# Four pair copies of Pool ahead of the last routing slot of a period

## The chip, the cores and the metric

The kernel runs on one core of one Trainium2 chip. The metric is the device time of one execution in microseconds (us): the median of several runs. TensorE (PE) multiplies matrices, VectorE (DVE), ScalarE (ACT) and Pool (GpSimd) work element by element, and the sync engine (SP) issues most transfers. Each engine runs its own list of instructions strictly in the order in which it was written, and waits at an instruction whose inputs aren't there yet.

## The reference

Attention inside chunks of 64 tokens, for 8 batches, 8 heads, 576 tokens and 64 values per head, and then a layer of 8 experts. Each token goes to one expert. Its own best one counts where a local gate is under one half; otherwise it takes over the expert of the token before it, so the choice is a running recurrence over the tokens of a batch.

```python
scores = scale * np.matmul(q_c, k_c.transpose(0, 1, 2, 4, 3))
attn = softmax(scores)                      # over the 64 keys of the chunk
x = np.matmul(attn, v_c)                    # then to (batch, token, 512)
...
for s in range(S):
    fresh_e = int(np.argmax(logits[b, s]))
    e = fresh_e if s == 0 or local_gate[b, s] < 0.5 else prev_e
    prev_e = e
    h = np.maximum(x[b, s] @ w1[e], 0.0)
    out[b, s] = p[e] * (h @ w2[e])          # p: softmax of the logits
```

## The kernel before

The 4608 tokens are cut into 18 blocks of 256 (numbers 0 to 17). Attention runs as a software pipeline over them. A *period* is one turn of the loop in line 754, with `i` from 1 to 15, and it works on several blocks at once, each at another stage. The order of the steps of a period is a string of tokens, `PAR["steady"]` in line 60; `play` (line 456) walks over it and issues what each token stands for. The lists of TensorE, VectorE, ScalarE and Pool all stand in exactly this order (`manual_schedule`, line 752), so a step of Pool that is written later runs later.

The tokens that matter here:

- `lq`, `lv`: SP issues the loads of `qt` and `kt` for block i+5 and of `v` for block i+1.
- `pr` (four steps, `a_pair`, line 433, through `pair_heads`): Pool copies `qt` and `kt` of block i+3 into `qr` and `kr`, pairing heads, in two copies each (line 156). `qr` and `kr` have a single buffer.
- `tq` (eight steps): TensorE transposes `qr` and `kr` of block i+2 (line 164), and ScalarE takes the results out of PSUM. So what `pr` of one period writes, `tq` of the next one reads.
- `ra` (two steps, `router`): the logits of block i-2, in lines 284 and 293, with VectorE in between; its last step writes the finished rows to the DRAM tensor `x_d` (line 302).
- `s`, `tp`, `va`, `tx`: scores and softmax, transposes of the probabilities, values (line 242), transposes of the output.
- `h0` to `h3`: four slots of a period, in which a step of the *routing* of the first 9 blocks can be placed.

The routing is the recurrence above for 18 tiles of 128 tokens at a time, then a rank for each token inside its expert, and then the slots that tokens take in the expert tiles. It consists of 18 steps. `PAR["hooks"]` gives each a number; the number divided by 4 is the period and the rest is the slot. So 59 is `h3` of period 14 and 63 is `h3` of period 15. In `h3` stand steps of VectorE or TensorE in periods 10 to 13. In period 14 stand `after_a` (lines 744 to 746, VectorE) and `onehots` (line 421): 18 one-hot matrices `rh`, of which VectorE makes every third and Pool the other twelve, as soon as VectorE has written the ranks `rq` (line 417) in slot `h2`. In period 15 stand the *slot matmuls* (line 559, 18 of them, which read `rh` and VectorE's `qv` of line 551) and the *early gather*: Pool issues three indirect transfers (line 594) that fetch rows of `x_d` for the first three expert tiles. Block 17 is the last, so `pr` does nothing in period 15.

At the end of each period from 8 to 15 Pool also makes one half of a low part of the first expert's weights (line 97), once ScalarE has made the high part.

After period 15 comes the *drain* (`PAR["drain"]`): the rest of attention, the routing of the other 9 blocks and the first three expert tiles, interleaved by hand in one order. Its token `x0` transposes the first gathered tile (line 588). Then follows the expert stage: 46 tiles at most of 128 tokens, each with 24 matmuls of 512 columns for `h` (line 627) and 24 for `y` (line 641).

```python
toks = [t for t in PAR["steady"].split() if opt.get(t.split("*")[0], 1) is not None]
play(" ".join(toks), qs4 | {k: v for k, v in opt.items() if v is not None})
...
dsts = [pe2.tile([P, 4, 2, 2, D], F32, name=nm + "r", tag=nm + "r", bufs=1) for nm in "qk"]
...
return [lambda t=t: rh_eng(t).tensor_scalar(rh[:, t], iota_m, rq[:, 0, t:t + 1], None, ALU.is_equal)
        for t in range(t0, t1)]
```

Of the kernel before, what the change touches and what calls it, by code (L numbers as in the profile page):

```python
# [56 lines left out]
    "t0": "VAVA",  # L57
    "t1": "AAAA",
    "t2": "AVAA",
    "steady": "lq s*8 s h0 tx*8 s va*4 va tq*8 ra*2 h1 tq*8 va*4 lv va ra*2 h2 tp*8 s h3 pr*4 ",  # L60
    "hooks": [43, 43, 46, 47, 49, 50, 51, 51, 53, 54, 55, 55, 58, 59, 59, 62, 63, 63],
}

# [918 lines left out]
```

## Time and profile before

| what | value |
|---|---|
| median of 3 runs | 723.87 us (723.59 to 726.48) |
| the profiled execution | 728.72 us |
| its span, first to last instruction | 726.9 us |
| mean granted TensorE clock | 0.969 of full speed |
| TensorE busy | 661.4 us, 91% of the span |
| Pool busy | 188.1 us, 26% of the span |
| moved by the DMA engines | 97.49 MB, 134 GB/s in the mean |

The profile is of one execution, and its timeline counts from the first instruction. A row of the timeline has the start, the duration, the engine, the line and operation, what is written and read, how many instructions were merged, and in brackets how long the engine sat idle before and what ended that. The periods spoken of below lie near 149 to 156 us (period 14) and 156 to 174 us (period 15), by the matmuls of line 193 with which each begins; the drain follows, and the expert stage fills TensorE from some 230 us on. A row of the windows has the stretch, its length, the busy time and count of each of TensorE's matmuls, its weight loads, VectorE, ScalarE and Pool, then the granted TensorE clock, the DMA engines' busy share and their GB/s.

### The profile page before, as it was taken

What the parts mean: (1) busy time and instruction counts of PE and PEld (TensorE: products, weight loads), DVE (VectorE), ACT (ScalarE), POOL (GpSimd) and SP (SyncE); (2) the same over time, 40 slices, a digit from 0 to 9 for tenths busy, and PEclk for the clock granted to TensorE, in tenths of its full rate; (3) what the DMA queues carried; (4) which work ended last, traced back from release to release, by engine and by line L of the source; (5) the groups of instructions that cost most, each with busy time, mean ns of one, the idle gap of its engine ahead of it and who ended that gap; (6) DMA issues with size and microseconds to landing.
All of it is one profiled execution on the core that took longest, in us unless ns stands there. A gap on an engine that the chain in (4) does not pass through costs nothing. (4 is left out here: it accounts for less than half of the span.)

```text
span 726.9 us, 17103 instructions
## 1 busy us (share of the span) xinstructions
PE 661.4 (91%) x5594; PEld 524.8 (72%) x5594; DVE 362.0 (50%) x852; ACT 272.2 (37%) x432; POOL 188.1 (26%) x230
## 2 busy tenths in 40 slices
PE   4779898777999999999999999999999999999971
PEld 4668676565777788777888887778877888777861
DVE  2547655574685585256232562572576323454310
ACT  3547665554521234341222443422454222432210
POOL 3322233345022132123121231331243212231100
PEclk9989999998999999999999999999999999999986
DMA  9999999996833144145111253441277111333100
GB/s 211 201 200 234 233 240 245 247 254 178 217 102 118 46 148 135 71 146 164 42 46 46 84 164 101 148 156 47 79 239 249 60 44 46 97 111 130 49 19 15
DMA packets 102928, 97.49 MB, mean 134 GB/s; under 512 B 42672, under 2 KB 79536, under 8 KB 102768
## 3 DMA queue, kind: packets, MB, share of 16 engines
q1 hardware_dynamic: 96608, 75.70, 42.1%
q0 software_dynamic: 6160, 19.85, 8.2%
q8 instruction: 78, 1.28, 0.8%
q14 instruction: 82, 0.67, 0.3%
HBM read 76.48 MB, written 19.56 MB: 132 GB/s over the span
## 5 line engine op out<-in xcount | busy, mean ns | idle before, releaser
L641 PE MATMUL y<-w2h,hp 128*128 128x512 f32 x608 | 203.7, 405 | 10.3 <-DVE hp L591 6.3
L627 PE MATMUL h<-w1h,xp 128*128 128x512 f32 x608 | 178.3, 403 | 0.0
L641 PEld LDWEIGHTS y<-w2h,hp 128*128 128x128 f32 x608 | 114.9, 190 | 39.1 <-DVE hp L591 8.9
L627 PEld LDWEIGHTS h<-w1h,xp 128*128 128x128 f32 x608 | 111.4, 189 | 23.9 <-ACTq L863 0.2
L641 PE MATMUL y<-w2l,hp 128*128 128x512 f32 x304 | 121.1, 399 | 0.0
L700 POOL DMA_INDIRECT out<-ysb,sidx x38 | 41.2, 1085 | 273.5 <-DVEq L863 197.4
L627 PE MATMUL h<-w1l,xp 128*128 128x512 f32 x304 | 95.9, 396 | 0.0
L590 ACT CAST hp<-tr 128x512 fp32r<-128x512 f32 x76 | 41.2, 589 | 108.0 <-PE tr L588 97.0
L591 DVE TENSOR_TENSOR xp<-tr,xp 128x512 fp32r<-128x512 f32 x39 | 27.0, 691 | 106.5 <-ACTq L863 67.0
L699 DVE TENSOR_SCALAR ysb<-y,ppr 128x512 f32<-128x512 f32 x35 | 26.2, 747 | 92.7 <-PE y L641 81.7
L627 PEld LDWEIGHTS h<-w1l,xp 128*128 128x128 f32 x304 | 57.0, 188 | 14.7 <-DVEq L863 0.7
L641 PEld LDWEIGHTS y<-w2l,hp 128*128 128x128 f32 x304 | 57.9, 190 | 12.3
L680 ACT ACTIVATE hsb<-h 128x1024 f32<-128x1024 f32 x35 | 35.9, 1027 | 67.5 <-PE h L627 64.9
L591 DVE TENSOR_TENSOR hp<-tr,hp 128x512 fp32r<-128x512 f32 x76 | 49.2, 685 | 13.5 <-ACT hp L590 12.5
L613 ACT ACTIVATE pex<-pex 128x8 f32<-128x8 f32 x38 | 7.9, 209 | 117.2 <-DVE pex L612 117.2
L594 POOL DMA_INDIRECT xg<-x_d,gidx x36 | 36.9, 1026 | 40.7 <-issue 19.3
L97 POOL TENSOR_TENSOR w1l<-raw,w1h 128x512 fp32r<-128x512 f32 (+1 forms) x15 | 27.7, 1844 | 70.6 <-ACT w1h L96 70.6
L242 PE MATMUL o<-v,pT 64*64 64x65 f32 x1152 | 32.0, 235 | 13.5 <-DMA v<-in_v 12.9
L242 PEld LDWEIGHTS o<-v,pT 64*64 64x64 f32 x1152 | 24.6, 143 | 23.0 <-DMA v<-in_v 15.8
L588 PE MATMUL tr<-ident,hsb 128*128 128x128 f32 x304 | 40.3, 273 | 0.3 <-ACT hsb L680 0.3
L97 DVE TENSOR_TENSOR w2l<-raw,w2h 128x1024 fp32r<-128x1024 f32 x21 | 39.9, 1952 | 0.9 <-issue 0.9
L588 PEld LDWEIGHTS tr<-ident,hsb 128*128 128x128 f32 x304 | 35.3, 141 | 6.8 <-ACT w2h L96 1.2
(173 smaller groups left out, 832.5 us busy)
## 6 DMA issues: line engine op xcount, KB each, us to landing
raw<-in_moe_w SPq DMA_DIRECT2D x72, 512.0 KB, 5.0
x_d<-xs SPq DMA_DIRECT2D x18, 521.0 KB, 5.7
v<-in_v SPq DMA_DIRECT2D x72, 128.0 KB, 6.0
qt<-in_q SPq DMA_DIRECT2D x11, 512.0 KB, 6.4
kt<-in_k SPq DMA_DIRECT2D x11, 512.0 KB, 7.6
qt<-in_q SPq DMA_DIRECT2D x6, 256.0 KB, 6.2
kt<-in_k SPq DMA_DIRECT2D x6, 256.0 KB, 6.7
qt<-in_q SPq DMA_DIRECT2D x4, 384.0 KB, 7.0
```

What stands on the lines that cost most here:

```text
L97: (lo_eng or nc.vector).tensor_tensor(lo, raw, hi.bitcast(F32), ALU.subtract)
L242: nc.tensor.matmul(o[64 * cp:64 * cp + 64, cc, DV * h:DV * h + D + 1], pT[64 * cc:64 * cc + 64, 4 * j + h, 64 * cp:64 * cp + 64], vt[64 * ...
L588: nc.tensor.transpose(ps[:, n], src_of(n), ident)
L590: return [tr, lambda: nc.scalar.copy(hi, box["ps"]), lambda: V.tensor_tensor(lo, box["ps"], hi.bitcast(F32), ALU.subtract)]
L591: lambda: V.tensor_tensor(lo, box["ps"], hi.bitcast(F32), ALU.subtract)]
L594: nc.gpsimd.indirect_dma_start(out=dst, out_offset=None, in_=src, in_offset=bass.IndirectOffsetOnAxis(ap=gidx[t].bitcast(U32), axis=0))
L613: lambda: nc.scalar.activation(ex[:, 0], ex[:, 0], AF.Exp),
L627: nc.tensor.matmul(hs[:, j], xs[a][:, c], W1[w][c][:, 512 * j:512 * j + 512], start=(c == 0 and n == 0), stop=(c == 3 and n == 2))
L641: nc.tensor.matmul(y, hx[f // 4][a][:, f % 4], W2[w][c][:, f % 2, :], start=(f == 0 and n == 0), stop=(f == 7 and n == 2))
L680: nc.scalar.activation(hsb, hs.rearrange("p j f -> p (j f)"), AF.Relu)
L699: either(mix, lambda: V.tensor_scalar(ysb, y, pr, None, ALU.mult), lambda: y_mixed(ysb, y, ym, pr))
L700: nc.gpsimd.indirect_dma_start(out=out, out_offset=bass.IndirectOffsetOnAxis(ap=sidx[t].bitcast(U32), axis=0), in_=ysb, in_offset=None, bo ...
```

## The change

In the string for a period the token `pr*4` is put ahead of `h3`. Nothing else is edited.

```diff
-    "steady": "lq s*8 s h0 tx*8 s va*4 va tq*8 ra*2 h1 tq*8 va*4 lv va ra*2 h2 tp*8 s h3 pr*4 ",
+    "steady": "lq s*8 s h0 tx*8 s va*4 va tq*8 ra*2 h1 tq*8 va*4 lv va ra*2 h2 tp*8 s pr*4 h3 ",
```

Pool's list from period 13's weight split (`w1l_76`, line 97) to that of period 14 (`w1l_77`) and the first early gather; `qr` and `kr` are the pair copies of block 17, `rh` the one-hots. It is the only piece of Pool's list that differs:

```order
 L97 TENSOR_TENSOR w1l_76<-raw_2_88,w1h_72 128x512
+L156 COPY qr<-qt 128x4x128 x2
+L156 COPY kr<-kt 128x4x128 x2
 L421 TENSOR_SCALAR rh<-iota_m,rq 128x128 x12
-L156 COPY qr<-qt 128x4x128 x2
-L156 COPY kr<-kt 128x4x128 x2
 L97 TENSOR_TENSOR w1l_77<-raw_3_89,w1h_73 128x512
 L594 DMA raw_0_86<-x_d,gidx_2942 128x521
```

The four copies have moved from behind the twelve one-hots to in front of them; the weight split and the gather stand where they stood.

TensorE's list has the same instructions in the same order. Its semaphore waits differ in period 15, at the slot matmuls of line 559, which read the one-hots `rh`; a rank of Pool's list that TensorE had already waited for need not be waited for again. The start of that piece:

```order
 L559 LDWEIGHTS rh [waits DVE_49]
 L559 MATMUL tr<-qv_0_2896,rh 128x12 [waits Activation_49]
-L559 LDWEIGHTS rh
+L559 LDWEIGHTS rh [waits Pool_49]
+L559 MATMUL tr<-qv_0_2896,rh 128x12
+L559 LDWEIGHTS rh [waits Pool_49]
 L559 MATMUL tr<-qv_0_2896,rh 128x12
```

Each of the twelve weight loads of a one-hot that Pool makes has now a wait for Pool of its own; before, `tq` of the same period had waited for the copies behind all of them. The lists of VectorE, ScalarE and SP have the same instructions in the same order.

## The prediction

> **What bounds the kernel now.** I read the page first, for the engine that carries the span, then the waits of TensorE, then the timelines of the engines named there, and last the granted clock around that place.
>
> ```profile
> PE 661.4 (91%) x5594; PEld 524.8 (72%) x5594; DVE 362.0 (50%) x852; ACT 272.2 (37%) x432; POOL 188.1 (26%) x230
> ```
>
> TensorE is busy for 91% of the span, and nothing else comes near. The chain of waits on the page holds under 2% of the span, so it names no culprit. What TensorE waited for does: first up to 174 us, then from there to the end.
>
> ```profile
> PE o L242 <- DMA v<-in_v: 8.3, 13, 1.2
> PE tr L164 <- POOL qr L156: 5.7, 1, 5.7
> PE tr L559 <- DVE qv L551: 1.2, 1, 1.2
> ...
> PE y L641 <- DVE hp L591: 6.3, 5, 1.8
> PE y L641 <- ACTq L884: 3.7, 1, 3.7
> PE tr L588 <- DMA raw<-x_d,gidx: 1.1, 1, 1.1
> ```
>
> The columns are the sum, the count and the longest. One wait stands out: 5.7 us, once, in front of the transposes of line 164, for Pool's copy into `qr`. From 174 us on the only wait for a transfer is the 1.1 us for the first early gather; the others are for engines whose own work follows TensorE's, and they shift with it.
>
> ```profile
> 260.00:700.00 440.00, 433.41 (x2132) 343.87 (x2130) 208.44 (x416) 149.73 (x226) 108.23 (x86) 1.00 0.33 106
> ```
>
> In the expert stage TensorE has work for 433.41 of 440 us at clock 1.00, with the DMA engines a third busy. Work that starts earlier there ends earlier: no later transfer or engine can take back what the attention stage gains.
>
> **Where the 5.7 us come from.** Pool's timeline, from period 13 to the gathers:
>
> ```profile
> 143.45 1.17 POOL L156 COPY qr<-qt 128x512 f32<-128x512 f32 x2 [3.97 <-issue]
> 146.50 1.17 POOL L156 COPY kr<-kt 128x512 f32<-128x512 f32 x2 [1.88 <-issue]
> ...
> 158.55 7.07 POOL L421 TENSOR_SCALAR rh<-iota_m,rq 128x128 bf16<-128x128 bf16 x12 [6.81 <-DVE qsA L744]
> 165.55 1.17 POOL L156 COPY qr<-qt 128x512 f32<-128x512 f32 x2
> 166.66 1.19 POOL L156 COPY kr<-kt 128x512 f32<-128x512 f32 x2
> 167.80 1.28 POOL L97 TENSOR_TENSOR w1l<-raw,w1h 128x512 fp32r<-128x512 f32 x1
> 175.45 1.19 POOL L594 DMA_INDIRECT raw<-x_d,gidx  x1 [6.37 <-DVE sidx L572]
> ```
>
> Pool sits idle for 6.81 us until VectorE has the ranks, makes twelve one-hots in 7.07 us, and only then does the pair copies of block 17, whose transposes TensorE wants in period 15. TensorE, first in period 14 and then in 15:
>
> ```profile
> 151.84 1.09 PE L164 MATMUL tr<-ident,qr 128*128 128x128 f32 x8
> 152.86 0.64 PE L284 MATMUL lg<-xT,wg 128*32 128x256 f32 x8
> 153.43 1.09 PE L164 MATMUL tr<-ident,kr 128*128 128x128 f32 x8
> ...
> 155.09 0.44 PE L293 MATMUL lg<-ident,lT 128*128 128x128 f32 x2
> ...
> 166.22 1.97 PE L164 MATMUL tr<-ident,qr 128*128 128x128 f32 x8 [5.71 <-POOL qr L156]
> 168.12 1.08 PE L284 MATMUL lg<-xT,wg 128*32 128x256 f32 x8
> 169.13 1.52 PE L164 MATMUL tr<-ident,kr 128*128 128x128 f32 x8
> ...
> 171.21 0.44 PE L293 MATMUL lg<-ident,lT 128*128 128x128 f32 x2
> ...
> 173.76 0.61 PE L559 MATMUL tr<-qv,rh 128*128 128x12 bf16 x18 [1.24 <-DVE qv L551]
> ```
>
> **The change, part by part.** Only Pool's order in period 14 changes: the four copies stand ahead of the twelve one-hots. In the other periods no Pool work stands at this place, or no copy does.
>
> *The stall goes: 5.71 us.* The copies need three things: the landed `qt` and `kt`, and `qr` and `kr` read out by period 14's transposes. Those reads end at 152.93 and 154.52. In period 13 the copy into `kr` at 146.50 followed the same kind of read by about 0.1 us, so I put the new copies at 153.1 to 154.2 and 154.6 to 155.8. The loads are long there:
>
> ```profile
> 139.60 0.43 SPq L125 DMA_DIRECT2D qt<-in_q  x1
> 140.12 1.05 SPq L125 DMA_DIRECT2D kt<-in_k  x1
> ...
> DMA to landing us min/median/max: 5.5/7.6/10.0
> ```
>
> By the slowest landing of a `kt` in this stretch (10.0 us) the second has landed by 151.2. So the copies end near 155.8, in the 6.81 us in which Pool waited anyway: the one-hots still start at 158.55 and end at 165.62, and cost nothing more. TensorE gets to the transposes at 166.22 - 5.71 = 160.51 and finds them fed.
>
> *The slow clock after the stall goes: 1.74 us.* From the first `qr` transpose to line 293 period 15 took 171.21 - 166.22 = 4.99 us, and period 14 took 155.09 - 151.84 = 3.25 us, for the same list of matmuls. The windows show why (the third number from the end is the granted clock):
>
> ```profile
> 150.00:160.00 10.00, 8.89 (x209) 7.23 (x202) 8.50 (x32) 6.74 (x12) 2.73 (x4) 1.00 1.09 272
> 160.00:163.00 3.00, 0.51 (x32) 0.37 (x28) 2.93 (x7) 0.62 (x2) 3.00 (x6) 1.00 1.31 198
> 163.00:170.00 7.00, 3.78 (x20) 2.64 (x21) 0.78 (x2) 1.26 (x2) 6.08 (x10) 0.52 0.70 211
> 170.00:175.00 5.00, 3.76 (x112) 3.27 (x113) 2.71 (x15) 3.68 (x6) 0.00 (x0) 0.99 0.35 79
> ```
>
> The clock drops to about half in the stall and is back near 170. Without the stall I give period 15 the 3.25 us of period 14. [...]
>
> *What is late next.* The sum is 5.71 + 1.74 = 7.45 us at line 293. Behind it the slot matmuls of line 559 waited 1.24 us for VectorE; VectorE's work there follows line 293, so this wait stays and they start at 173.76 - 7.45 = 166.31. They read the one-hots, which end at 165.62: 0.7 us to spare, and I count no wait. But the covering wait is gone. Before, the wait for the later pair copies also said that the one-hots were done; now twelve weight loads wait for Pool one by one. No row has such a wait on TensorE when it is already satisfied; the nearest is a satisfied one of VectorE:
>
> ```profile
> L156 DVEq EVENT_SEMAPHORE  x2: 21/21/21, 5.9 to 20.2; - x2
> ```
>
> Bounds are 0 and the whole duration of the 18 matmuls once more (0.61 us); twelve times 21 ns is 0.25 us, and I take that.
>
> *The transfers get closer together.* Line 137's load of `v` for block 16 and line 302's write follow TensorE, so they move up with it.
>
> ```profile
> 161.71 1.95 SPq L93 DMA_DIRECT2D raw<-in_moe_w  x2
> 171.29 2.67 SPq L137 DMA_DIRECT2D v<-in_v  x4
> ...
> 154.00:168.00 14.00, 7.18 (x159) 6.06 (x157) 7.88 (x29) 5.32 (x9) 9.45 (x17) 0.83 1.05 269
> 168.00:171.00 3.00, 3.00 (x44) 1.90 (x47) 0.42 (x1) 1.38 (x4) 1.08 (x1) 0.66 0.03 11
> 171.00:182.00 11.00, 8.26 (x203) 6.96 (x196) 7.69 (x27) 6.58 (x12) 4.37 (x4) 1.00 0.68 183
> ...
> 180.90 0.63 PE L588 MATMUL tr<-ident,raw 128*128 128x128 f32 x4 [1.06 <-DMA raw<-x_d,gidx]
> ```
>
> Before, the DMA engines were saturated to 168 (269 GB/s), then empty for 3 us. After, `v` is issued at 171.29 - 7.45 = 163.84, into that backlog. Up to 182 there are 11 us at 183 GB/s to move, 2.0 MB; at 269 GB/s they need 7.5 us, and from 168 to the shifted 182 - 7.45 there are 6.6. So some 0.9 us are missing in the worst case that all of it must be there by then. Pool issues the first gather at 175.45 - 7.45 = 168.0, behind its weight split, which then ends near 166.9. TensorE's wait for it was 1.06 us. It can vanish (a gain of 1.06) or grow by the 0.9; a full queue is nearer to the second, and I take 0.5 us of loss.
>
> *Pool beside VectorE.* The copies now run beside VectorE's work of period 14, not alone, and more of VectorE's work falls beside the end of the one-hots. The copies of all periods, most of which ran so, and the twelve one-hots:
>
> ```profile
> L156 POOL COPY kr<-kt x35: 608/617/629, 7.3 to 167.2; 128x512 f32<-128x512 f32 x35
> ...
> L421 POOL TENSOR_SCALAR rh<-iota_m,rq x12: 597/604/641, 158.5 to 165.0; 128x128 bf16<-128x128 bf16 x12
> ```
>
> No copy took over 629 ns and no one-hot over 641: nothing to add. Twelve at 641 would take 7.7 us and end 0.6 later, still inside the margin. [...]
>
> **The sum.** 5.71 + 1.74 - 0.25 - 0.5 = 6.7 us. The profiled execution took 728.72 us (span 726.9): it would take 722.0. The median of the runs is 4.85 us lower, 723.87; the stall is one between engines and should be in those runs too, so I take the same 6.7 us off: **717.2 us**.
>
> **The rivals.** *The transfers take half of it back.* The gather lands behind the backlog and TensorE's wait grows from 1.06 to about 2.9 us (the 0.9 above, and as much for its own bytes in a full queue); that wait could let the clock drop once more, for another 1.74 us. It keeps 7.45 - 0.25 - 1.8 - 1.7 = 3.7 us: 720.2. For it: the 13 waits for `v` in the busy stretch before. Against it: from 160.5 to 163 TensorE was idle and the clock still 1.00, so 2.9 us is barely enough. Chance 0.13.
>
> *The one-hots become the wait.* If VectorE's work slows each by 0.15 us, they end 1.8 us later than 165.62, and line 559 waits 1.1 us: 718.3. It bites from 0.7 us on. Chance 0.08. Against it: the row above.
>
> *Nothing is gained.* Period 15's transposes wait for something that ended just before the copies did, or a new wait as long as the old comes in the drain: 723.9. Nothing in the waits shows one. Chance 0.04.
>
> *Slower.* The copies now stand ahead of the one-hots, so what holds the copies up holds those up, the weight split and the early gathers behind them, and TensorE at line 559 instead of line 164. If `kt` for block 17 landed so late that the copies ended at T, the one-hots would end at T + 7.07 and the slot matmuls would start no earlier. It costs nothing up to T = 159.2, and the gain is gone at T = 166.7; for 4 us above before (727.9) T would be 170.7, a landing over 28 us after the issue, against 10.0 at most. Chance 0.02.
>
> **How the numbers follow.** The forecast has 0.73: TensorE gains 6 to 8 us. The best end is the vanished gather wait and free semaphores, 7.45 + 1.06 = 8.5 us, 715.4; the runs of before lie up to 2.6 us apart, so I go to 714.8. The upper end takes in the first rival, 720.4. About 0.5% (3.6 us) is what a measurement can tell from no change; that is 720.25, which the first rival straddles. Faster: 0.73 + 0.08 + two thirds of 0.13, about 0.90; within: 0.08; slower: 0.02.
>
> **What would show it.** After the change the timeline should have Pool's copies for block 17 near 153 and 154.6, one-hots still from about 158.5; no wait of line 164 for Pool in period 15; a clock of 1.00 from 160 to 167; the slot matmuls near 166.3; the first early gather near 168, and the wait at line 588 at 0 to 2 us. I am wrong if the copies wait beyond 158, if line 559 waits for Pool, if the clock falls again between 166 and 176, or if the drain gains a wait for `v`.

## The result, and the profile after

| | before | changed |
|---|---|---|
| median of 16 runs each | 725.38 us | 721.67 us |
| lowest, highest | 722.57, 727.40 us | 717.21, 724.28 us |
| ratio of the changed kernel, 95% interval | | 0.9945 [0.9925, 0.9965] |
| the same in a later timing (17 and 9 runs) | 726.53 us | 720.03 us, 0.9929 [0.9900, 0.9959] |
| profiled execution, its span | 728.72, 726.9 us | 721.68, 719.9 us |

The kernel is faster by 0.35 to 0.75%, some 4 us, and not by the 6.7 us of the forecast; 721.67 us lies above the range. The two profiled spans differ by 7.0 us, which looks like the forecast. It isn't: 4.2 us of that lie ahead of period 14, where both kernels are the same. Only a stretch between two points of the program that stand around the change says what the change did.

The engines' line of the page of after (busy time, share of the span, instructions):

```profile
PE 658.9 (92%) x5594; PEld 523.3 (73%) x5594; DVE 363.2 (50%) x852; ACT 271.7 (38%) x432; POOL 187.9 (26%) x230
```

TensorE is still the engine that is busy nearly all the time, and the others have the same work as before. The change is in the waits. Pool's timeline after, from period 14's pair copies to the gathers:

```profile
149.61 1.17 POOL L156 COPY qr<-qt 128x512 f32<-128x512 f32 x2 [2.13 <-issue]
151.20 1.18 POOL L156 COPY kr<-kt 128x512 f32<-128x512 f32 x2 [0.43 <-POOL qr L156]
155.13 7.05 POOL L421 TENSOR_SCALAR rh<-iota_m,rq 128x128 bf16<-128x128 bf16 x12 [2.75 <-DVE qsA L744]
162.15 1.26 POOL L97 TENSOR_TENSOR w1l<-raw,w1h 128x512 fp32r<-128x512 f32 x1
166.00 1.19 POOL L594 DMA_INDIRECT raw<-x_d,gidx  x1 [2.59 <-DVE sidx L572]
```

The copies sit where they were forecast, between the reads of `qr` and `kr` and the ranks, though some 0.8 us later in the period than forecast, and Pool still has 2.75 us to spare before the one-hots. TensorE from the start of period 15 (152.88) into the drain:

```profile
152.88 1.16 PE L193 MATMUL sc<-kT,qT 64*64 64x64 f32 x64
...
155.62 1.09 PE L164 MATMUL tr<-ident,qr 128*128 128x128 f32 x8
156.65 0.64 PE L284 MATMUL lg<-xT,wg 128*32 128x256 f32 x8
157.22 1.09 PE L164 MATMUL tr<-ident,kr 128*128 128x128 f32 x8
160.00 0.70 PE L242 MATMUL o<-v,pT 64*64 64x65 f32 x32 [1.69 <-DVE xs L256]
160.63 0.44 PE L293 MATMUL lg<-ident,lT 128*128 128x128 f32 x2
...
164.32 0.61 PE L559 MATMUL tr<-qv,rh 128*128 128x12 bf16 x18 [2.38 <-DVE qv L551]
164.86 1.16 PE L193 MATMUL sc<-kT,qT 64*64 64x64 f32 x64
...
171.81 0.50 PE L242 MATMUL o<-v,pT 64*64 64x65 f32 x17 [0.87 <-issue]
...
172.76 0.63 PE L588 MATMUL tr<-ident,raw 128*128 128x128 f32 x4 [0.18 <-DMA raw<-x_d,gidx]
```

In brackets, `issue` means that the profile shows nothing for which the engine waited. The wait for Pool is gone. Two waits for VectorE are there instead: 1.69 us for the norm of line 256, which wasn't there, and 2.38 us for `qv`, which was 1.24. VectorE's rows in that place:

```profile
155.33 1.19 DVE L421 TENSOR_SCALAR rh<-iota_m,rq 128x128 bf16<-128x128 bf16 x6
156.44 1.28 DVE L204 TENSOR_REDUCE mx<-sc 128x8 f32<-128x512 f32 x2
157.64 1.27 DVE L207 TENSOR_TENSOR pr<-sc,mx 128x512 f32<-128x512 f32 x2
...
159.25 0.69 DVE L256 TENSOR_TENSOR xs<-o,rs 128x512 f32<-128x512 f32 x1
...
161.86 0.22 DVE L299 TENSOR_REDUCE L<-lg 128x18 f32<-128x72 f32 x1
162.12 1.32 DVE L301 COPY xs<-L 128x18 f32<-128x18 f32 x1
```

VectorE comes to the softmax of period 15 (line 204) only at 156.44, 3.56 us into the period, behind the ranks and its own six one-hots; its norm ends at 159.94. And its copy of 18 values a row, in line 301, takes 1.32 us. It ends at 163.44, 0.03 us after Pool's weight split (162.15 + 1.26 = 163.41).

The windows of the same stretch; the third number from the end is the clock:

```profile
160.00:162.00 2.00, 1.94 (x42) 1.63 (x42) 1.39 (x5) 0.46 (x1) 2.00 (x4) 1.00 1.21 273
162.00:164.00 2.00, 0.00 (x0) 0.00 (x0) 1.97 (x7) 2.00 (x4) 1.41 (x2) 1.00 0.99 300
164.00:166.00 2.00, 1.68 (x83) 1.59 (x83) 1.14 (x8) 0.07 (x1) 0.00 (x0) 1.00 1.12 315
166.00:168.00 2.00, 2.00 (x19) 1.43 (x16) 1.77 (x3) 0.58 (x1) 1.69 (x2) 0.56 1.42 145
168.00:170.00 2.00, 2.00 (x32) 1.67 (x31) 0.84 (x4) 0.63 (x1) 1.67 (x3) 0.58 1.18 224
170.00:172.00 2.00, 1.08 (x31) 0.73 (x33) 0.94 (x2) 1.91 (x4) 1.01 (x1) 1.00 1.03 378
```

The clock stays at 1.00 through period 15, as forecast, but drops to about half from 166 to 170, behind the two waits; the DMA engines are saturated throughout (share 0.99 to 1.42), where before they had been empty from 168 to 171 (0.03).

### The profile page after: what moved, and what is told of

Same layout as the page of the kernel before. It is cut to its first block, busy times and chain, and to the rows that moved or that the text cites. A ratio compares the mean times of both kernels' runs of the same rounds, so it can differ in the third digit from the quotient of the medians.

```text
span 719.9 us, 17103 instructions
## 1 busy us (share of the span) xinstructions
PE 658.9 (92%) x5594; PEld 523.3 (73%) x5594; DVE 363.2 (50%) x852; ACT 271.7 (38%) x432; POOL 187.9 (26%) x230
## 5 line engine op out<-in xcount | busy, mean ns | idle before, releaser
L242 PE MATMUL o<-v,pT 64*64 64x65 f32 x1152 | 33.2, 233 | 17.5 <-DMA v<-in_v 13.9
```

The source lines that it names most:

```text
L242: nc.tensor.matmul(o[64 * cp:64 * cp + 64, cc, DV * h:DV * h + D + 1], pT[64 * cc:64 * cc + 64, 4 * j + h, 64 * cp:64 * cp + 64], vt[64 * ...
```

## The experiments

All runs are compared by the same points: the first score matmul of period 14 (line 193), that of period 15, line 293 and line 559 in it, the score matmuls of block 17, the first transpose of a gathered tile (line 588) and the first matmul of line 641. Other runs' numbers are read off their timelines at these points.

**More profiles of the two kernels.** Runs before_again, after_again, before_third and after_timed are the two kernels unedited.

> The kernel before once more, for a second look. Stage meant in all runs: from the first score matmul of period 14 (line 193) to the first transpose of a gathered tile (line 588); it was 180.90 - 149.10 = 31.8 us before and 172.76 - 144.86 = 27.9 us after, 3.9 us less, while the two spans differ by 7.0 us. Theory A (the rest of the 7.0 us is drawn anew in each execution, in the transfer-bound periods ahead of period 14 and by where the clock drops): the stage is again 31 to 32.5 us with the one wait for Pool of 5 to 6.5 us, while period 14 begins 1 us or more away from 149.1. Rival (the change moved something ahead of period 14): period 14 begins within 0.5 us of 149.1.

> The changed kernel once more. Theory A: the stage from period 14 to line 588 is again 27 to 29 us, period 14 begins anywhere within some 4 us. In period 15 TensorE again waits 1 to 2 us for VectorE's xs (line 256) and over 2 us for qv (line 551), and no more for Pool. Rival (these two waits were chance): they are gone or under 0.5 us and 1.3 us, and the stage is 25.5 us or less.

> The kernel before a third time, because its two profiled executions (728.7 and 731.0 us) lie above nearly all of its timed runs and begin period 14 at 149.1 and 148.5, against 143.9 to 146.2 in the four executions with the copies in front. Theory A (chance in the transfer-bound start): period 14 begins near 145 here and the execution takes some 725 us, the stage from period 14 to line 588 is 31 to 33 us. Rival (something makes the kernel before slower ahead of period 14): it begins at 148 or later again.

> The changed kernel timed in the same call as the two below, as their base. Theory A: ratio to before 0.993 to 0.9955; from period 14 (first score matmul of line 193) to the first matmul of line 641 it takes 52 to 53.5 us, against 56.8 to 58.2 in three executions of the kernel before.

| us, three executions each | before | changed | difference of the means |
|---|---|---|---|
| start of period 14 | 149.10, 148.50, 146.06 | 144.86, 145.86, 148.51 | |
| period 14 to 15 | 7.23, 8.50, 8.14 | 8.02, 8.10, 7.30 | -0.15 |
| period 15 to line 293 | 14.89, 15.55, 15.77 | 7.75, 7.72, 7.72 | -7.67 |
| line 293 to 559 | 2.55, 2.55, 2.55 | 3.69, 3.72, 3.71 | +1.16 |
| line 559 to block 17's scores | 0.54, 0.54, 0.54 | 0.54, 0.54, 0.54 | 0.00 |
| from there to line 588 | 6.59, 6.04, 6.15 | 7.90, 7.50, 8.48 | +1.70 |
| line 588 to 641 | 25.01, 25.01, 25.01 | 25.02, 25.02, 26.57 | +0.53 |
| period 14 to line 641 | 56.81, 58.19, 58.15 | 52.92, 52.60, 54.30 | -4.44 |

The start of period 14 moves by up to 3.7 us between executions of one kernel, so Theory A holds in this. Its ranges don't all hold: the stall in before_again is 7.07 us, period 14 to line 588 takes 33.2 us there and 33.1 us in before_third, and after_timed takes 54.30 us to line 641. The stretch around the change gains 4.44 us in the mean, which is what the timed runs show (0.55 to 0.71% of 725.4 to 726.5 us is 4.0 to 5.2 us). The wait for `qv` is 2.4 us in all three; that for `xs` is 1.69, 1.65 and, behind a late start of TensorE by 1.13 us, 0.26 us.

**Pool's weight split away from VectorE's copy.** In run defer Pool's half of the split of period 14 waits until the gathers are issued:

```diff
-            split(w1h[c][:, col], w1l[c][:, col], raw1[c][:, col], nc.gpsimd)
+            if i == 14:
+                held = (w1h[c][:, col], w1l[c][:, col], raw1[c][:, col])
+                nc.scalar.copy(held[0], held[2])
+            else:
+                split(w1h[c][:, col], w1l[c][:, col], raw1[c][:, col], nc.gpsimd)
+            if i == 15:
+                nc.gpsimd.tensor_tensor(held[1], held[2], held[0].bitcast(F32), ALU.subtract)
```

> The changed kernel with Pool's weight split of period 14 issued behind that of period 15 (behind the early gathers). Theory B (VectorE's copy of line 301 took 1.32 us and not 0.18 us because Pool's two-input split of line 97 ran at the same time): the copy takes under 0.3 us, line 559 waits 1.1 to 1.4 us for qv and not 2.4, the stage shortens by 1.1 us, and by up to 2.5 us if the slow clock behind it goes too; ratio to before 0.991 to 0.994. Rival (a slow write or a transfer held that copy up): it takes over 1 us again, no change of the stage, ratio 0.9945.

VectorE's copy and TensorE's line 559 in it:

```profile
161.56 0.18 DVE L301 COPY xs<-L 128x18 f32<-128x18 f32 x1
...
162.62 0.61 PE L559 MATMUL tr<-qv,rh 128*128 128x12 bf16 x18 [1.24 <-DVE qv L551]
```

The copy is back at 0.18 us and the wait at 1.24. Line 293 to 559 takes 2.55 us, as before the change. So that copy was held up by Pool's split (1.32 us beside it, 0.18 without it), and this is worth 1.16 us at that place. Run no_v_onehots, of the next group, has the split in place and shows how: there the copy begins 0.23 us behind the split, takes 1.06 us, and again ends 0.03 us after it. At the end defer brings little: period 14 to line 641 takes 52.42 us, against 52.60 to 54.30, the ratio is 0.9935 [0.9912, 0.9959]. The half clock came later, at 170.4, and there was a wait of 1.02 us for the gather.

**VectorE's queue.** In no_v_onehots VectorE's six one-hots aren't made, and Pool fills all of `rh` with zeros at the start; in v12 (on top of defer) it makes twelve and Pool six; in rank57 its rank steps stand one slot earlier.

```diff
# no_v_onehots
+    nc.gpsimd.memset(rh[:, 0:TA], 0.0)
-                    for t in range(t0, t1)]
+                    for t in range(t0, t1) if t0 or t % 3]
# v12
-    sg, sg_rank, sg_onehots = route(0, TA, lambda t: nc.gpsimd if t % 3 else nc.vector)
+    sg, sg_rank, sg_onehots = route(0, TA, lambda t: nc.gpsimd if t % 3 == 1 else nc.vector)
# rank57
-    "hooks": [43, 43, 46, 47, 49, 50, 51, 51, 53, 54, 55, 55, 58, 59, 59, 62, 63, 63],
+    "hooks": [43, 43, 46, 47, 49, 50, 51, 51, 53, 54, 55, 55, 57, 59, 59, 62, 63, 63],
```

> The changed kernel without VectorE's six one-hots of the first routing; a third of the one-hots stays zero, so the early tiles get wrong rows and are partly not written. Theory C (VectorE's routing work, queued ahead of the softmax, is what TensorE waits for in period 15): VectorE's first reduction of period 15 starts 1.1 us earlier against TensorE's scores, the wait for xs falls from 1.7 us to 0.4 to 0.7. Rival (the wait comes from x_d's transfer freeing xs, or from TensorE's own pace): it stays above 1.2 us.

> The run with the deferred weight split, with twelve one-hots of the first routing on VectorE and six on Pool, so VectorE has 1.1 us more ahead of the softmax of period 15. Theory C: the end of VectorE's first norm in period 15 (line 256) lies 8.1 to 8.2 us behind the first score matmul of the period, against 7.03 to 7.07 in all earlier runs with the six one-hots at this place, and TensorE's wait for xs is 1.1 us longer than the 1.7 us of the changed kernel (less by what TensorE loses to late instructions before it). Rival (that wait comes from x_d or TensorE's own pace): 7.0 to 7.1 us and a wait up to 1.8 us.

> The changed kernel with the seven rank steps (lines 411 to 417) in slot h1 of period 14 and not h2, so some 2 us of VectorE's work leaves the place behind period 14's last norm. Theory C (with the copies in front, period 15 is bound by VectorE, which enters it late by the routing of period 14): TensorE's wait for xs in period 15 falls from 1.7 us to under 0.5, the one-hots start 2 us earlier, line 559 starts 2 to 2.5 us earlier, no slow clock in the drain; stage 24.5 to 26 us, ratio to before 0.988 to 0.992. Rival (transfers bound this stretch after the change: 1.1 to 1.4 DMA share): other waits, for v or x_d, take their place and the stage stays within 0.7 us of 27.9; ratio 0.994 to 0.996.

TensorE's waits of no_v_onehots, and then the rows of v12 (TensorE's first matmul of the period, VectorE's one-hots and norm, TensorE's wait):

```profile
PE sc L193 <- issue: 1.7, 1, 1.7
...
PE o L242 <- DVE xs L256: 0.3, 1, 0.3
```

```profile
153.25 1.16 PE L193 MATMUL sc<-kT,qT 64*64 64x64 f32 x64
...
155.68 2.45 DVE L421 TENSOR_SCALAR rh<-iota_m,rq 128x128 bf16<-128x128 bf16 x12
...
160.87 0.69 DVE L256 TENSOR_TENSOR xs<-o,rs 128x512 f32<-128x512 f32 x1
...
161.61 0.87 PE L242 MATMUL o<-v,pT 64*64 64x65 f32 x32 [2.93 <-DVE xs L256]
```

The first can't decide: the wait for `xs` fell to 0.3 us, but TensorE had lost 1.7 us just ahead of it, in which VectorE catches up anyway. v12 decides: 1.26 us more of VectorE's work (2.45 against 1.19) put the end of the norm at 161.56, 8.31 us into the period against 7.06, and the wait from 1.69 to 2.93 us, by as much. VectorE's queue sets it. Yet v12 takes 52.40 us from period 14 to line 641, no more than defer: by these two profiles, the end of the stretch doesn't hang on this wait. In rank57 the one-hots start 2.0 us earlier and the norm ends 6.35 us into the period, but the wait falls only to 0.95 us: VectorE has too little free time in period 14 to take the ranks, and its last norm of period 14 ends 1.20 us into period 15 and not 0.08. Line 559 starts 1.85 us earlier in the period than in the changed kernel, but the drain takes that back, period 14 to line 641 takes 52.86 us, and the ratio is 0.9948 [0.9928, 0.9968].

**The routing earlier still.** Run early, on top of defer, moves the routing's steps ahead by up to three slots:

```diff
-    "hooks": [43, 43, 46, 47, 49, 50, 51, 51, 53, 54, 55, 55, 58, 59, 59, 62, 63, 63],
+    "hooks": [43, 43, 45, 46, 47, 49, 50, 50, 51, 53, 53, 54, 55, 57, 59, 61, 63, 63],
```

> The run with the deferred weight split, and in it the routing's steps moved ahead by one to three slots each: the ranks to the end of period 13, VectorE's first slot step to h1 of period 15. Periods 11 to 13 are those in which TensorE waits for v, so VectorE has time there. Theory C: the one-hots start near 152 us by the clock of the changed kernel's profile, 3 us ahead; the wait for xs in period 15 falls under 0.5 us and that for qv under 0.3; stage 23.5 to 25 us, ratio to before 0.988 to 0.992. Rival (what VectorE gains is taken back by the same list of VectorE in periods 13 and 14, or by transfers): period 13 to 14 gets longer by as much, ratio 0.9935 as with the split alone.

In period 15 the waits for `xs` and `qv` are gone: line 293 to 559 takes 1.15 us. But period 14 takes 10.17 us and not 7.3 to 8.1, with a wait of 1.9 us for VectorE there, and a shorter one at the end of period 13:

```profile
PE o L242 <- DVE xs L256: 2.2, 2, 1.9
...
PE tr L390 <- DVE oh L385: 1.2, 1, 1.2
```

So the rival holds: the same work of VectorE is waited for a period earlier. Period 14 to line 641 takes 52.48 us, the ratio is 0.9932 [0.9905, 0.9960].

**Transfers.** In w2late the loads of the second half of w2 (1 MB of the first expert's second weight matrix) are issued at the end of period 15; in w2drain, on top of defer, in the drain behind the last `v`.

```diff
# w2late
-        if i in (13, 14):
-            for c in range(2 * i - 26, 2 * i - 24):
+        if i in (13, 15):
+            for c in range(i - 13, i - 11):
# w2drain
-        if i in (13, 14):
+        if i == 13:
...
+    def ld():
+        vts[n] = load_v(n)
+        load_w2(0, 2)
+        load_w2(0, 3)
-        s=lambda: sa, ld=load(vts, load_v, n), rt=lambda: sb, rk=sb_rank, of=lambda: offsets, oh=sb_onehots,
+        s=lambda: sa, ld=lambda: [ld], rt=lambda: sb, rk=sb_rank, of=lambda: offsets, oh=sb_onehots,
```

> The changed kernel with the loads of the second half of w2 (1 MB) issued at the end of period 15 and not of period 14. Theory D (after the change the DMA engines are the bound from 150 to 172 us: late instruction fetches, waits for v, x_d and the gather): the waits of TensorE marked issue and the waits for v and x_d go, the stage shortens by 1 to 2 us; ratio to before 0.990 to 0.993. Rival, theory C (VectorE bounds it): waits for xs and qv stay at 1 to 1.7 and 2.4 us, stage 27 to 28 us, ratio 0.9945.

> The run with the deferred weight split, and in it the loads of the second half of w2 (1 MB) issued in the drain, behind the load of v for block 17, so they are no longer in front of the early gathers. Theory D2 (behind the change transfers set the drain's start): the first gathered tile lands 3.8 to 4.4 us after its issue, no issue wait at line 242 in the drain, period 14 to the first matmul of line 641 takes 50 to 51.3 us (52.4 with the split alone), ratio to before 0.988 to 0.992. Rival (the short waits and the half clock set it, whatever the transfers): 52.3 to 53 us, with a slow stretch of 3.4 us between 160 and 180; or TensorE and ScalarE wait for the late w2 instead.

In w2late the two waits for VectorE stay, and the wait for the gather grows to 1.8 us (0.18, 0.59 and 1.4 in the changed kernel), with the megabyte now issued just ahead of it:

```profile
PE tr L559 <- DVE qv L551: 2.4, 1, 2.4
PE o L242 <- DVE xs L256: 2.0, 2, 1.7
PE tr L588 <- DMA raw<-x_d,gidx: 1.8, 1, 1.8
```

Period 14 to line 641 takes 55.24 us in the profile; the timed ratio is 0.9915 [0.9882, 0.9948], and its interval overlaps with those of the changed kernel. The profile has half clock twice, from 164.7 and from 175.0. w2drain has no wait for the gather and no wait marked issue above 0.21 us in the drain, and its timed ratio is what was expected, 0.9902 [0.9872, 0.9931]; but in its profile the stretch took 55.31 us, with 2.5 us of waits for `v` in period 14 and again a half clock at 174.9. One execution doesn't settle it.

**Line 588 later, and TensorE kept busy.** Run x0late (on top of defer) puts the transposes of the first gathered tile behind seven others; warm adds 16 transposes of the identity to period 15 of that, in the places of the two waits; w2drain_warm has warm and w2drain together.

```diff
# x0late
-        "... tx3 va2 s va2*2 tp0 x0 "
-        "va2 x0 tp0*4 tp0*4 ld va1 ..."
+        "... tx3 va2 s va2*2 tp0 "
+        "va2 tp0*4 tp0*4 x0*2 ld va1 ..."
# warm
+    def idle(k):
+        ps = trp().rearrange("p (n t) -> p n t", n=4)
+        for n in range(4 * k):
+            nc.tensor.transpose(ps[:, n % 4], ident, ident)
+        if i == 15:
+            toks = " ".join(toks).replace("tq*8 va*4 lv va", "tq*8 dz va*4 lv va").replace("tp*8 s h3", "tp*8 s dy h3").split()
+            qs4 |= dict(dz=lambda: [lambda: idle(2)], dy=lambda: [lambda: idle(2)])
```

> The run with the deferred weight split, and in it the transposes of the first gathered tile (line 588) seven transposes later in the drain. Theory E (behind the change the end of the gather's transfer sets the drain's pace: it landed 4.4 to 6.3 us after its issue in the changed order against 3.8 to 4.3 before, and TensorE waited 1.0 to 1.8 us for it wherever it came earlier): the wait at line 588 is 0 to 0.8 us, period 14 to the first matmul of line 641 takes 51 to 52 us (52.4 with the split alone), ratio to before 0.990 to 0.993. Rival (the slow clock or late instructions take it instead): 52.3 to 53 us again, with a slow stretch of 3.4 us between 160 and 180.

> The run before with 16 transposes of the identity added in period 15, eight where TensorE waits for xs and eight where it waits for qv; their results are not used. Theory F (the 3.4 us of half clock that each changed execution has between 165 and 177 come from these short waits added up, and cost 1.4 us): no slow stretch between 155 and 178, period 14 to the first matmul of line 641 is 50 to 51 us, ratio 0.988 to 0.991. Rival (the added work costs what it saves, or the clock falls anyway by the later waits): a slow stretch remains, time within 0.7 us of the run without the transposes or longer.

> The 16 added transposes once more. Theory F: without a late fetch of several us there is no slow stretch between 155 and 178, and period 14 to the first matmul of line 641 takes 49.5 to 51 us. Rival: again 52.3 to 53 us.

> Both: the added transposes and w2's second half loaded in the drain. If transfers and clock both count: 49 to 50.5 us for the stage, ratio to before 0.986 to 0.990. If one of them is a mere place at which the same time is lost: as the better of the two alone.

In x0late nothing waits for the gather any more, and another wait stands a few matmuls ahead of it:

```profile
172.21 0.50 PE L242 MATMUL o<-v,pT 64*64 64x65 f32 x17 [1.87 <-issue]
```

The stretch takes 52.93 us, with the half clock at 173.0: the rival. warm took 52.84 us. It had its half clock earlier, from 158.7 to 162.1, right behind a wait of 3.0 us marked issue, and none from there to 690. warm_again, the same kernel, took 53.26 us and had the half clock at 173.5, among other waits of 0.2, 0.4 and 1.2 us. So Theory F falls: filling the two waits of period 15 doesn't keep the clock up. Timed, x0late has 0.9911 [0.9877, 0.9945] and warm 0.9923 [0.9894, 0.9952]. w2drain_warm is the fastest version by its ratio, 0.9890 [0.9855, 0.9926]. Its profile has no half clock between 144 and 300 us, and still 52.29 us in the stretch: in the drain ScalarE now waits 3.6 us for the late w2, and TensorE 1.1 and 1.2 us for VectorE. It beats the kernel before clearly; its interval overlaps with those of the changed kernel, so it isn't shown to beat that one.

## Why the prediction was wrong

**The base.** The forecast took 723.87 us as the time before, the median of three runs. In 16 runs it is 725.38, and 725.28 to 727.67 in the later timings. That is 1.5 of the 4.5 us between 717.2 and 721.67. The other 3.0 are gain that didn't come: 6.7 forecast, 3.7 between these medians. The three profiles of the stretch put the gain at 4.4, and the later timing at 5.2.

**"The stall goes: 5.71 us" and "the slow clock after the stall goes: 1.74 us": right in the sum, in part by luck.** Period 15 to line 293 got shorter by 7.67 us, against 7.45. The copies, the one-hots, the missing wait and the clock of 1.00 up to line 293 are as forecast. But "I give period 15 the 3.25 us of period 14" was wrong: from 155.62 to 160.63 it takes 5.01 us, as long as before, with 1.69 us of waiting where there had been a slow clock. The profile before had it. VectorE's norm there ends 7.02 us into period 15, but 4.75 us into period 14; the stall had hidden the difference. The sum came out because VectorE sets line 293 at 7.72 to 7.75 us whether or not TensorE loses 1 us earlier in the period, as it had in the execution that the forecast was made from. A missed wait and that loss, which the forecast had left in, nearly cancel.

**"VectorE's work there follows line 293, so this wait stays": the first step that failed.** The wait doubled, 1.16 us. The one-hots now end while VectorE works, so Pool's two-input split behind them falls on VectorE's copy. The forecast put the copies and the one-hots beside VectorE and found no price. It moved the split up for the gather's sake only and didn't put it beside VectorE's work, and it looked for a price on Pool's instructions alone, while VectorE paid. Run defer shows the price: 1.32 us beside the split, 0.18 without it. That VectorE's work slows the one-hots, by the 0.15 us each of the second rival, no run shows: the twelve took 7.05 us, and 7.07 before.

**The twelve new waits: nothing**, against 0.25 us: line 559 to the scores takes 0.54 us in all six executions.

**"A full queue is nearer to the second, and I take 0.5 us of loss": the second step that failed, in size.** The wait for the gather hardly grew (0.18, 0.59 and 1.4 us, against 1.1 and 0.5 and one execution without it), but the drain up to line 641 lost 2.2 us (1.70 + 0.53). In each of the three executions there is one stretch of 3.4 us at half clock between 166 and 180, and in two a wait marked issue. TensorE is busy throughout each such stretch, so it should cost some 1.7 us (an estimate: half of its length). The sum had nothing for a half clock after the stall; that the clock would fall between 166 and 176 stood among the signs of being wrong. It fell without a wait as long as the old stall: in the 3.4 us ahead of the three falls TensorE was busy for 57, 39 and 25% of the time, and no single wait of TensorE from 150 to 195 us was over 2.41 us (more on this in the last section). The first rival, transfers taking back half of the gain with the clock falling once more, came closest: it gave 3.7 us of gain. Its mechanism, one long wait for the gather, isn't what the trace shows.

Together: 1.16 + 2.23 us lost against 0.75 forecast, and 7.67 + 0.15 gained against 7.45, make 4.4 instead of 6.7.

**What stays open.** How the drain's loss divides exactly between the clock, the waits marked issue and transfers, and how to get it back. From block 17's scores to line 641 the kernel before took 31.1 to 31.6 us and the changed kernel 32.5 to 35.1; v12 and warm, whose half clock came ahead of these scores, took 31.3 and 30.8, which speaks for the clock as a large part of it. But nearly all variants end with 52.3 to 53.3 us from period 14 to line 641, whichever wait was taken out; the delays took each other's place.

## What to carry to other kernels

A stall of one engine is time for all others: before counting it as gain, list what each of them still did during it, on the engine that the stalled one needs next above all, and see when that would end without the stall. When an instruction moves, look at what follows it on its engine too; it moves as well, and may fall beside work that it holds up (here Pool's split beside VectorE's copy, 1.32 us and not 0.18). Compare two profiles by points around the change, not by their spans, and take the base from many runs.

## What the hardware showed unexpectedly

- A VectorE copy of 128x18 values took 1.32, 1.35, 1.34 and 1.32 us, and not 0.18, in four runs (after, after_again, after_timed, w2late) in which Pool's two-input operation of 1.26 us began at nearly the same time. It ended with Pool's instruction, and so it did where it began 0.23 us later (1.06 us, no_v_onehots).
- TensorE's waits marked issue come at fixed places of its list, in sizes from 0 to 3.0 us; behind 62 of the 64 score matmuls of period 15 such a wait was 1.11 us in before, 0.49 in defer and 1.13 in after_timed. Of 42 above 0.3 us in the first 230 us of the 17 traces, 41 follow a transfer of 16 KB in an instruction queue that had landed 1.2 to 2.0 us before. In before and after they are five, and the transfer had landed 1.3 to 1.6 us before TensorE went on. The expectations call these waits late instructions or a late fetch; that is the author's estimate, and no run tried it alone.
- The half clock came without one long wait too. In each of the 17 traces the stretches of half clock begin on one grid of 3.41 us and last one or several whole windows of it (all 77 of them between 30 and 690 us); in the first trace of before they begin at 47.18, 91.55, 112.03, 142.75 and 163.23 us, in that of after at 46.79, 166.26 and 538.31. Of the windows at full clock in which TensorE was busy for less than half, 51 of 53 were followed by half clock (5 of 5 in these two traces); of those in which it was busy for 60% or more, 1 of 3050 (0 of 364); in between, 25 of 74 (3 of 8). Two windows of after_again, one behind the other:

```profile
163.33:166.74 3.41, 1.34 (x70) 1.32 (x74) 2.62 (x12) 1.80 (x3) 1.16 (x1) 1.00 1.12 280
166.74:170.15 3.41, 3.41 (x58) 2.51 (x52) 2.16 (x6) 1.22 (x2) 2.45 (x3) 0.50 1.26 217
```

So the clock fell to half behind waits of 1 to 2.4 us as well. The busy share of one window doesn't decide it alone: in the first profile after, two windows running, from 159.43 and 162.85 us, had 57% each, and only the second was followed by half clock.
